# Taking the mean of a weight matrix from the float32 blocks as loaded, in a fused retention and expert kernel

## The chip, the cores and the metric

The kernel runs on one core of one Trainium2 chip. The metric is the device time of one execution in microseconds (us). The engines are called PE (TensorE, the matrix engine; PEld is its loading of weights), DVE (VectorE), ACT (ScalarE), POOL (GpSimd) and SP (SyncE, which here only issues transfers).

## The reference

Two stages. The first is a retention layer over q, k and v of 8 batches, 8 heads, 576 positions and 64 dimensions: scores with a causal decay mask, times v, no softmax. The second takes its output x (4608 tokens by 512) through an expert layer:

```python
scores = scale * np.matmul(q, k.transpose(0, 1, 3, 2))
ret = scores * Dmat[None, :, :, :]          # Dmat = gamma_h ** (i - j), causal
x = np.matmul(ret, v)                        # -> [4608, 512]
h = x @ w_in                                 # w_in 512 x 1024
e = np.exp(h - h_max)
solu = h * (e / np.sum(e))
ln = (solu - mu) / np.sqrt(var + 1e-06) * g_ln
out = ln @ w_out                             # w_out 1024 x 512
```

The subtraction of mu in front of w_out is folded into the weights: with W = g_ln * w_out (rows scaled), the kernel multiplies by W minus the mean of W over its 1024 rows. Finding this mean is what the change is about.

## The kernel before

The work is cut into 36 items i (a window of 256 positions by four heads, or the short last windows of four batches together) and 36 token tiles t of 128 tokens; two items make two tiles. Every step has a short name, and a number for its item, tile or block:

- SP: ldq, ldk, ldv load an item (256 KB each); lwi0 to lwi3 load the four blocks of w_in and lwo0, lwo2, lwo4, lwo6 the four double blocks of w_out (512 KB each) into a pool of five float32 buffers, wst; out stores a tile.
- sq, sk scale q and k by the decay into f16, cv casts v. They are on POOL, but for a few of the first items, which are on DVE or ACT.
- PE: T transposes q and k of an item, K multiplies k by v (the state), S makes the scores, I and V the output of the item. ACT copies T's result with Te (or TL) and the output with xe. DVE takes up the state with st and masks the scores with mask. POOL carries the state on with sm and sc.
- Tile t: M1 on PE (eight products into h_ps, one buffer of two PSUM banks), ex on ACT (exponential with its sum), so on DVE (h times e), L on PE (transposes), Le or TL on ACT, M2 on PE (eight products with w2c), oe on ACT, out. The statistics are bnA, bnB on DVE, or va on ACT with fin on DVE for the first four tiles; fx on ACT and rs on POOL make the factor of each row.
- Weights: wi0a to wi3b cast w_in into f16, half on ACT, half on DVE. For w_out, wg0 to wg7 make scaled f16 copies (g times the block), four on ACT (L714) and four on DVE (L710). WM (L720) multiplies them on PE by a constant f16 matrix `minus` of -1/1024, eight f16 products that add up in PSUM: every partition then holds minus the mean row. wc0 to wc7 on DVE (L728) read the float32 block again, scale it by g, add the mean from PSUM and write the centred f16 weights w2c over the scaled copies. M2_0 is the first that needs all eight wc. The PSUM bank of WM is that of the first four L (buffer `tl1[1]`), so L2 waits until the last wc has read it.

A setting of the plan, WE, says whether the mean is first copied from PSUM to SBUF by ACT (step wm, L724) and read from there by wc. It is 0 before:

```python
    op("WM", "PE", "WM", [f"wg{x}" for x in range(8)], (4, 1.3), [("tlL", ["wm"] if WE else [f"wc{x}" for x in range(8)])])
            op(f"wc{x}", "DVE", "wc", ["wm" if WE else "WM", f"lwo{c}"], (4, 0.1 * x))
```

The order on each engine is fixed in the program. A planner inside the kernel (plan, order_ops, with its own table of durations and due times) sorts the steps, and two tables, FIRST and LAST, give the order of the head and of the end by hand. PE's head before begins so:

```python
        "T0 S0 K0 K1 T1 I0 S1 V0 I1 V1 M1_0 K2 T2 T3 K3 S2 M1_1 I2 S3 V2 L0 I3 V3 T4 L1 K4 S4 M1_2 K6 WM K5 "
        "M1_3 T5 K7 T6 I4 S5 V4 T7 I5 S6 V5 T8 M1_4 I6 S7 V6 K8 T9 L2 M2_0 I7 L3 V7 K9 S8 M1_5 M2_1 I8 L4 V8 "
```

Where the planner expects PE to idle in the head, it puts in products of zeros (L846), 45 of them, which keep PE busy. At the end, cnt, cs and ci count the rows whose sum of exponentials lies in a safe range, and a branch on that count either finishes the last half tile or runs a general, slow version; with these data it is never the slow one.

Of the kernel before, what the change touches and what calls it, by code (L numbers as in the profile page):

```python
# [17 lines left out]
for _b in range(0, B, 4):  # L18
# [5 lines left out]
    T=0.26, L=0.26, Tw=0.45, Lw=0.45, I=0.22, V=0.23, K=0.13, S=0.22, M1=1.73, M2=1.73, M2h=0.87, oeh=0.42, G=0.1, WM=1.73,  # L24
# [3 lines left out]
    ldx=0.88, ldw=1.36, out=0.65,  # L28
# [4 lines left out]
NJ, NK, LAG, WE = 8, 8, 6, 0  # L33
VA = (0, 1, 2, 3)
ON = {'sq0': 'DVE', 'sq1': 'DVE', 'cv0': 'ACT', 'cv1': 'ACT', 'sk2': 'DVE', 'sk3': 'DVE', 'cv2': 'ACT', 'cv3': 'ACT', 'cv4': 'ACT', 'cv5': 'ACT', 'cv6': 'ACT', 'cv7': 'ACT'}
CAP = dict(
    rawq=5, rawk=5, rawv=5, q16=3, k16=4, v16=4, ev=8, s=1, ret=2, xy=1, gg=6, gt=2, s160=4, s161=9, h=1,
# [11 lines left out]
    ),  # L49
    ACT=(  # L50
# [4 lines left out]
    ),  # L55
    DVE=(
# [5 lines left out]
    ),  # L62
    POOL=(
# [4 lines left out]
    ),  # L68
    SP=(
# [13 lines left out]
        "oe27 xe34 ex32 Le30 Le31 oe28 xe35 ex33 fx15 oe29 ex34 Le32 oe30 Le33 oe31 fx16 ex35 oe32 Le34 oe33 "  # L83
        "Le35 fx17 oe34 oe35 oz"
    ),
    DVE=(
        "so31 mask35 bnA31 so32 bnB31 bnA32 so33 bnB32 so34 bnA34 bnA33 bnB33 bnB34 cnt so35 bnA35 ci bnB35"
# [5 lines left out]
        "out27 out28 out29 out30 out31 out32 out33 out34 out35"  # L93
# [28 lines left out]
def plan():  # L122
# [42 lines left out]
    for t in range(NT):  # L165
# [20 lines left out]
        op(f"L{t}", "PE", "Lw" if early else "L", [f"so{t}"] + after, (m + 2, 0.1),  # L186
# [5 lines left out]
        op(f"M2_{t}", "PE", "M2h" if end else "M2", need, (t + LAG, 3.1), [("h" if end else "xy" if late(t) and t % 2 else "s", [f"oe{t}"])])  # L192
# [116 lines left out]
def kernel(  # L309
# [44 lines left out]
    minus = const.tile([P, P], F16)  # L354
# [3 lines left out]
    se = const.tile([P, NT], FP)  # L358
# [222 lines left out]
    def mm1(t):  # L581
        w, c = divmod(t, 2)
        tk[t]["h"] = h_ps = pools["h"].tile([P, DFF], FP, tag="h", name="h_ps")
        for half in range(2):
            hh = slice(half * 512, half * 512 + 512)
            for dc in range(4):
# [5 lines left out]
    def exp_(t):
        d = tk[t]
        d["e"] = pools["e"].tile([P, DFF], FP, tag="e", name="e_sb")
        nc.scalar.activation(out=d["e"], in_=d["h"], func=ACT.Exp, accum_out=se[:, t : t + 1])  # L595

    def solu(t):
        d = tk[t]
        w, c = divmod(t, 2)
        d["solu"] = pools["solu"].tile([P, DFF], F16, tag="solu", name="solu")  # L600
        if c == 0:
            ws[w]["mv"] = pools["sml"].tile([P, 2, 2], FP, tag="mv", name="mv")
        if t in VA:
            d["su"] = pools["sml"].tile([P, 1], FP, tag="su", name="su")
            nc.vector.scalar_tensor_tensor(
                out=d["solu"], in0=d["h"], scalar=1.0, in1=d["e"], op0=ALU.mult, op1=ALU.mult,
                accum_out=d["su"],
            )
        else:
            nc.vector.tensor_tensor(out=d["solu"], in0=d["h"], in1=d["e"], op=ALU.mult)  # L610
# [9 lines left out]
    def squares(t):  # L620
# [4 lines left out]
            out=x, in_=d["solu"], func=ACT.Square, bias=d["su"], scale=-1024.0,  # L625
# [82 lines left out]
    def w2_cast(x, eng):  # L708
        if eng == "DVE":
            nc.vector.tensor_scalar(  # L710
                out=w2c16[:, x], in0=w2_f(x), scalar1=gln[:, x : x + 1], scalar2=None, op0=ALU.mult
            )
# [248 lines left out]
```

## Time and profile before

| | us |
|---|---|
| median of 3 runs | 213.53 (213.11 to 214.47) |
| the profiled execution, its own time | 212.58 |
| its span in the profile | 210.9 |
| PE busy | 200.8 (95%), 4400 instructions |
| DVE busy | 166.1 (79%) |
| ACT busy | 141.7 (67%) |
| POOL busy | 141.7 (67%) |
| of PE: products of zeros | 13.7 |
| first M1 / first M2 starts | 15.6 / 45.25 |

Rows of groups read: line, engine, operation, output<-inputs, shapes, count | busy us, mean ns of one | idle time of the engine before them. Rows of time read: start, length, engine, line, operation, with the idle time before it and what ended it in brackets. Rows of windows read: stretch, then busy time and number of instructions of each engine, the granted clock of PE, the share of the transfer engines and GB/s. In the slices, each digit is a fortieth of the span in tenths.

### The profile page before, as it was taken

To read this page: it belongs to the slowest core of one execution; us is meant where nothing else is said; L and a number is where in the kernel's file an instruction comes from. 1 tells how busy PE (TensorE), PEld (TensorE's weight loads), DVE (VectorE), ACT (ScalarE), POOL (GpSimd) and SP (SyncE) were. 2 spreads that over 40 slices of the span, in tenths; PEclk is the share of its full clock that TensorE was granted. 3 is DMA by queue.
4 is the path that set the end of the run, shared out by engine and by line. 5 is a ranking of instruction groups with operands and counts; after the bars stand their busy time and mean duration, and the time that the engine had idled before them with its cause. 6 is when DMAs were issued, how large, how long until landed. Compare 5 with 4: busy or idle time off the path is not lost. (4 is left out here: it accounts for less than half of the span.)

```text
span 210.9 us, 10171 instructions
## 1 busy us (share of the span) xinstructions
PE 200.8 (95%) x4400; PEld 113.2 (54%) x4400; DVE 166.1 (79%) x279; ACT 141.7 (67%) x235; POOL 141.7 (67%) x240
## 2 busy tenths in 40 slices
PE   7986989999999999999999999999999999999992
PEld 2442654665566555555555555555666555554451
DVE  6565779997868898978898898889988998753760
ACT  2375787897666776776666777666767777573752
POOL 7434758999997975948787979797979792001110
PEclk9999999999999999999999999999999999999999
DMA  5999999999666559778999686776355222311224
GB/s 157 345 355 334 329 311 269 301 293 306 195 188 188 169 139 278 217 214 259 314 288 305 198 252 183 217 234 181 94 152 153 54 57 67 71 63 54 101 101 104
DMA packets 64814, 42.66 MB, mean 202 GB/s; under 512 B 3320, under 2 KB 58624, under 8 KB 64768
## 3 DMA queue, kind: packets, MB, share of 16 engines
q1 hardware_dynamic: 64528, 41.82, 68.4%
q8 instruction: 34, 0.56, 1.2%
q10 hardware_dynamic: 240, 0.18, 0.5%
q14 instruction: 12, 0.10, 0.2%
HBM read 32.55 MB, written 9.44 MB: 199 GB/s over the span
## 5 line engine op out<-in xcount | busy, mean ns | idle before, releaser
L587 PE MATMUL h_ps<-w_in,xT 128*128 128x512 f16 x288 | 68.5, 380 | 0.0
L660 PE MATMUL o_ps<-w2c,ev 128*128 128x512 f16 (+1 forms) x296 | 67.6, 373 | 0.0
L610 DVE TENSOR_TENSOR solu<-h_ps,e_sb 128x1024 f16<-128x1024 f32 x32 | 39.2, 1223 | 16.7 <-ACT e_sb L595 16.5
L595 ACT ACTIVATE e_sb<-h_ps 128x1024 f32<-128x1024 f32 x36 | 36.8, 1023 | 21.9 <-PE h_ps L587 20.4
L540 DVE TENSOR_TENSOR ret<-s_ps,masks 128x1024 f16<-128x1024 f32 x36 | 43.9, 1220 | 6.0 <-PE s_ps L508 5.4
L660 PEld LDWEIGHTS <-ev 128*128 128x128 f16 x296 | 28.7, 98 | 32.7
L616 DVE BATCH_NORM_STATS2 bs<-solu 128x6 f32<-128x512 f16 x64 | 43.6, 685 | 0.9
L587 PEld LDWEIGHTS <-xT 128*128 128x128 f16 x288 | 25.3, 98 | 29.1 <-ACT xT L576 0.8
L394 POOL TENSOR_TENSOR q<-rawq,small 128x512 f16<-128x512 f32 x34 | 35.4, 1042 | 7.3 <-DMA rawq<-in_q_dram 5.9
L669 ACT ACTIVATE o_sb<-o_ps,rs 128x512 f32<-128x512 f32 (+1 forms) x37 | 25.0, 676 | 21.8 <-PE o_ps L660 10.4
L394 POOL TENSOR_TENSOR k<-rawk,small 128x512 f16<-128x512 f32 x34 | 35.4, 1042 | 6.0 <-DMA rawk<-in_k_dram 5.9
L457 ACT COPY ev<-tl 128x1024 f32<-128x1024 f32 (+1 forms) x32 | 29.7, 932 | 4.7 <-PE tl L429 4.2
L576 ACT CAST xT<-xy 128x512 f16<-128x512 f32 x36 | 26.7, 742 | 3.0 <-PE xy L472 2.9
L571 POOL CAST sbd<-gg 64x256 f16<-64x256 f32 x64 | 25.4, 397 | 3.0
L562 POOL TENSOR_TENSOR gg<-gt,small 128x128 f32<-128x128 f32 x32 | 13.1, 409 | 16.9 <-DVE gt L557 16.5
L648 POOL TENSOR_TENSOR w<-mv,w 128x2 f32<-128x2 f32 x16 | 3.1, 194 | 27.8 <-ACT w L633 13.9
L399 POOL CAST v<-rawv 128x512 f16<-128x512 f32 x28 | 17.1, 609 | 0.2
L508 PE MATMUL s_ps<-ev 64*64 64x128 f16 x576 | 14.8, 218 | 0.3
L472 PE MATMUL xy<-ret,v 64*64 64x128 f16 x576 | 14.7, 217 | 0.0
L472 PEld LDWEIGHTS <-sbd 128*128 128x128 f16 x128 | 9.3, 98 | 9.3 <-issue 1.1
L446 PE MATMUL tl<-ident,solu 64*64 64x64 f16 x1024 | 14.2, 195 | 0.0
L846 PE MATMUL tl<-zeros 128*128 128x512 f16 x41 | 12.7, 445 | 1.3 <-DVE zeros L802 1.3
(71 smaller groups left out, 214.6 us busy)
## 6 DMA issues: line engine op xcount, KB each, us to landing
rawq<-in_q_dram SPq DMA_DIRECT2D x32, 256.0 KB, 5.1
rawk<-in_k_dram SPq DMA_DIRECT2D x32, 256.0 KB, 5.3
rawv<-in_v_dram SPq DMA_DIRECT2D x32, 256.0 KB, 5.1
out_dram<-o_sb SPq DMA_DIRECT2D x26, 256.0 KB, 3.1
out_dram<-o_sb SPq DMA_DIRECT2D x19, 128.0 KB, 2.3
wst<-in_moe_w_in_dram SPq DMA_DIRECT2D x4, 512.0 KB, 6.8
wst<-in_moe_w_out_dram SPq DMA_DIRECT2D x4, 512.0 KB, 7.1
rawq<-in_q_dram SPq DMA_DIRECT2D x16, 64.0 KB, 2.4
```

The lines of the kernel that those rows point to most:

```text
L394: eng.tensor_tensor(out=t.rearrange("p j h d -> p h j d"), in0=st[i]["r" + nm], in1=g, op=ALU.mult)
L457: nc.scalar.copy(out=t[:, lo:hi].rearrange("p x (r w) -> p r x w", r=2), in_=tls[n].rearrange("p r x w -> p (r x w)").bitcast(FP).rearrang ...
L472: nc.tensor.matmul(start=(c, e) not in begun, stop=False, skip_group_check=True, **kw)
L540: nc.vector.tensor_tensor(out=d["ret"].rearrange("p e h j q -> p (e h) (j q)"), in0=d["s"].rearrange("p e h j q -> p (e h) (j q)"), in1=ma ...
L571: nc.gpsimd.tensor_copy(out=t[ee[e], :, :, ee[e]], in_=st[i]["gg"][ee[e]])
L576: nc.scalar.copy(out=xT[:, 2 * w : 2 * w + 2, 2 * hf : 2 * hf + 2].rearrange("p c h (q j) -> p c h j q", j=2), in_=xys[i][:, :, 0:256].rea ...
L587: nc.tensor.matmul(out=h_ps[:, hh], lhsT=xT[:, t, dc], rhs=w_in16[:, dc, hh], start=(dc == 0), stop=(dc == 3),)
L595: nc.scalar.activation(out=d["e"], in_=d["h"], func=ACT.Exp, accum_out=se[:, t : t + 1])
L610: nc.vector.tensor_tensor(out=d["solu"], in0=d["h"], in1=d["e"], op=ALU.mult)
L616: nc.vector.bn_stats(out=d["bs"][:, half], in_=d["solu"][:, half * 512 : half * 512 + 512])
L660: nc.tensor.matmul(out=o, lhsT=d["ev"][:, d["lo"] + c], rhs=w2c16[:, c, mm], start=(c == 0), stop=(c == 7))
L669: nc.scalar.activation(out=d["osb"][:, mm], in_=d["o", half], func=ACT.Copy, scale=ws[t // 2]["rs"][:, t % 2 : t % 2 + 1])
```

## The change

The scaled copies wg go, all eight, and so does the constant `minus`. In their place one DVE instruction, gn, writes a float32 matrix g_neg: for each of the eight blocks, g times -1/1024 repeated over 128 columns. WM becomes eight separate steps WM0 to WM7, each a float32 product of g_neg's block with the float32 block of w_out as loaded, so that each can run as soon as its own load has landed; they are spread over the head of PE's order. WE becomes 1: ACT copies the mean to SBUF (wm), and wc reads it there. cv8 and cv9 move from POOL to ACT. h_ps is now one fixed buffer with its two halves known to the plan. Code that splits the first tiles' M1, ex and so into halves comes in as well, with its settings at 0 (NH, HX, ND). All the hand-written orders are new: among others the w_out loads stand earlier in SP's, L2 and L3 earlier in PE's, so35 ahead of cnt at the end, and 33 products of zeros are left instead of 45. In the changed kernel's own numbering the lines are some 43 higher.

```diff
-NJ, NK, LAG, WE = 8, 8, 6, 0
+NH, HX, ND = 0, 0, 0
+NJ, NK, LAG, WE = 8, 8, 6, 1
+WO = (0, 2, 4, 6)
...
 FIRST = dict(
     PE=(
+        "K0 T0 S0 K1 T1 I0 S1 V0 I1 V1 M1_0 WM0 K2 WM1 T2 WM2 M1_1 WM3 K3 S2 T3 WM4 WM5 I2 S3 V2 T4 WM6 I3 S4 "
+        "V3 WM7 K4 M1_2 K5 T5 K6 L0 T6 I4 S5 V4 M1_3 S6 K7 L1 T7 I5 V5 L2 I6 S7 V6 K8 T8 M1_4 L3 T9 M2_0 I7 "
...
     ACT=(
+        "cv0 Te0 cv1 Te1 wi0a xe0 wi1a wi3a xe1 wi2a cv2 ex0 Te2 cv3 ex1 Te3 va0 xe2 Te4 cv4 xe3 wm cv5 cv6 "
...
     DVE=(
-        "sq0 sq1 st0 mask0 st1 wi1b mask1 wi2b wi3b wi0b sk2 sk3 st2 so0 st3 wg5 mask2 mask3 so1 st4 wg7 wg1 "
-        "wg3 mask4 st6 so2 st5 wc4 wc0 wc7 wc1 st7 so3 mask5 wc5 wc2 wc6 mask6 wc3 mask7 fin0 st8 so4 mask8 "
+        "sq0 st0 sq1 mask0 st1 wi0b mask1 wi3b gn wi2b wi1b sk2 st2 so0 sk3 st3 mask2 so1 mask3 mask4 st4 wc6 "
+        "wc2 st5 wc3 st6 so2 mask5 wc5 wc0 st7 wc4 mask6 so3 wc1 wc7 mask7 fin0 st8 so4 bnA4 mask8 st9 bnB4 "
...
     POOL=(
-        "sk0 sk1 sm0 sc0 sm1 sc1 sq2 sq3 sm2 sc2 sm3 sc3 sk4 sq4 sk6 sm4 sc4 sk5 sm6 sk7 sm5 sq5 sc5 sq6 sq7 "
-        "sk8 sq8 sk9 sc6 cv8 sq9 sm7 sc7 rs0 sq10 cv9 sq11 sm8 cv11 sk10 sc8 cv10 sk11 rs1 sm9 sc9 sq12 sm10 "
+        "sk0 sk1 sm0 sc0 sm1 sc1 sq2 sm2 sc2 sq3 sk4 sq4 sm3 sc3 sq5 sk5 sm4 sk6 sq6 sc4 sm5 sk7 sq7 sm6 sc5 "
+        "sc6 sq8 sk8 sm7 sk9 sq9 sc7 rs0 sm8 sq10 cv10 cv11 sc8 sq12 sk10 sq11 sk11 sm9 sk12 sc9 rs1 sm10 "
...
     SP=(
-        "ldq0 ldk0 ldv0 ldv1 ldq1 ldk1 lwi1 lwi2 lwi0 lwi3 ldk2 ldv2 ldq2 ldk3 ldq3 ldv3 lwo4 lwo0 ldk4 ldq4 "
-        "ldv4 lwo6 ldk6 lwo2 ldv6 ldk5 ldv5 ldk7 ldq5 ldv7 ldq6 ldk8 ldq7 ldq8 ldk9 ldv8 ldq9 ldq10 ldv9 "
+        "ldv0 ldk0 ldq0 ldk1 ldq1 ldv1 lwi0 lwi1 lwi3 lwi2 lwo0 ldk2 ldv2 ldq2 lwo2 ldv3 ldk3 ldq3 lwo4 ldk4 "
+        "ldq4 lwo6 ldv4 ldk5 ldq5 ldv5 ldv6 ldk6 ldq6 ldk7 ldq7 ldv7 ldq8 ldk8 ldv8 ldk9 ldq9 ldv9 ldq10 "
...
     DVE=(
-        "so31 mask35 bnA31 so32 bnB31 bnA32 so33 bnB32 so34 bnA34 bnA33 bnB33 bnB34 cnt so35 bnA35 ci bnB35"
+        "so31 bnA31 mask35 so32 bnB31 so33 bnA32 bnA33 so34 bnA34 bnB33 bnB32 bnB34 so35 cnt bnA35 ci bnB35"
...
-            op(f"wg{x}", "DVE" if x % 2 else "ACT", dict(DVE="wgD", ACT="wg"), [f"lwo{c}", "gc"], (1, 1.0 + 0.1 * x))
+    for n in range(8):
+        op(f"WM{n}", "PE", "WM", ["gn", f"lwo{WO[n // 2]}", f"WM{n - 1}" if n else ""], (3, 0.3 * n),
+           [] if n else [("tlL", ["wm"] if WE else [f"wc{x}" for x in range(8)])])
+    op("gn", "DVE", "gn", ["gc"], (-9999, 0.2))
...
-    minus = const.tile([P, P], F16)
+    g_neg = const.tile([P, 8, P], FP)
+    h_ps = pools["h"].tile([P, DFF], FP, tag="h", name="h_ps")
...
+    def g_neg_():
+        nc.vector.tensor_scalar(
+            out=g_neg, in0=gln[:, :, None].to_broadcast([P, 8, P]), scalar1=-1.0 / DFF, scalar2=None, op0=ALU.mult
+        )
...
-        for x in range(8):
-            nc.tensor.matmul(out=t, lhsT=minus, rhs=w2c16[:, x], start=(x == 0), stop=(x == 7))
+        x = WO[n // 2] + n % 2
+        nc.tensor.matmul(out=t, lhsT=g_neg[:, x], rhs=w2_f(x), start=(n == 0), stop=(n == 7))
```

More of the change, by code (lines that the diff above doesn't have):

```diff
@@ L32 @@
 OFF = 6.0
[L33 removed]
+NH, HX, ND = 0, 0, 0
+NJ, NK, LAG, WE = 8, 8, 6, 1
+WO = (0, 2, 4, 6)
 VA = (0, 1, 2, 3)
[L35 removed]
+ON = {'sq0': 'DVE', 'sq1': 'DVE', 'cv0': 'ACT', 'cv1': 'ACT', 'sk2': 'DVE', 'sk3': 'DVE', 'cv2': 'ACT', 'cv3': 'ACT', 'cv4': 'ACT', 'cv5': 'ACT', 'cv6': 'ACT', 'cv7': 'ACT', 'cv8': 'ACT', 'cv9': 'ACT'}
 CAP = dict(
[L37 removed]
+    rawq=5, rawk=5, rawv=5, q16=3, k16=4, v16=4, ev=8, s=1, ret=2, xy=1, gg=6, gt=2, s160=4, s161=9, ha=1, hb=1,
     e=2, solu=4, osb=3, tl=1, tlx=2, tlT=1, tlL=1, wst=5,
@@ L168, in plan @@
         va = t in VA
-        op(f"M1_{t}", "PE", "M1", [f"xe{2 * w}", f"xe{2 * w + 1}"] + [f"wi{x}{y}" for x in range(4) for y in "ab"], (m, 1.4), [("h", [f"so{t}"])])
-        op(f"ex{t}", "ACT", "ex", [f"M1_{t}"], (m, 3.3), [("e", [f"so{t}"])])
-        op(f"so{t}", "DVE", "soA" if va else "so", [f"ex{t}"], (m, 4.56), [("solu", [f"L{t}", f"va{t}" if va else f"bnB{t}"])])
+        xs = [f"xe{2 * w}", f"xe{2 * w + 1}"] + [f"wi{x}{y}" for x in range(4) for y in "ab"]
+        out = f"sp{t}" if t < NH else f"so{t}"
@@ L172, in plan @@
+        sums = t < HX or t < NH and va
+        if sums and c:
+            op(f"sg{w}", "POOL", "sg", ([f"ey{t - 1}", f"ey{t}"] if t < HX else []) + ([f"sp{t - 1}", f"sp{t}"] if va else []), (m, 4.9))
         if va:
-            op(f"va{t}", "ACT", "va", [f"so{t}"], (m + 1, 0.8))
+            op(f"va{t}", "ACT", "va", [f"sg{w}" if sums else out], (m + 1, 0.8))
         else:
-            op(f"bnA{t}", "DVE", "bnA", [f"so{t}"], (m + 1, 0.9))
+            op(f"bnA{t}", "DVE", "bnA", [out], (m + 1, 0.9))
@@ L218, in locks @@
 def locks(o):
-    return o.eng == "DVE" and o.name[:2] in ("sq", "sk", "cv", "wi", "wg")
+    return o.eng == "DVE" and o.name[:2] in ("sq", "sk", "cv", "wi", "gn")
 def parts(name):
@@ L579, in x_ev, with mm1 @@
         )
[L581 to L586, printed above, removed]
+    halves = [slice(0, 512), slice(512, 1024)]
+    def mm1(t, hs, dcs=range(4)):
+        for hh in hs:
+            for dc in dcs:
                 nc.tensor.matmul(
-                    out=h_ps[:, hh], lhsT=xT[:, t, dc], rhs=w_in16[:, dc, hh],
-                    start=(dc == 0), stop=(dc == 3),
-                )
@@ L592, in exp_ @@
[L592 to L597, printed above, removed]
+                    out=h_ps[:, hh], lhsT=xT[:, t, dc], rhs=w_in16[:, dc, hh], start=(dc == 0), stop=(dc == 3)
+                )
+    def exp_(t, half=0):
+        if not half:
+            tk[t]["e"] = pools["e"].tile([P, DFF], FP, tag="e", name="e_sb")
+        hh = halves[half] if t < HX else slice(0, DFF)
+        acc = part[:, 0, t, half : half + 1] if t < HX else se[:, t : t + 1]
+        nc.scalar.activation(out=tk[t]["e"][:, hh], in_=h_ps[:, hh], func=ACT.Exp, accum_out=acc)
@@ L598, in solu @@
+    def solu(t, half=0):
         d = tk[t]
         w, c = divmod(t, 2)
-        d["solu"] = pools["solu"].tile([P, DFF], F16, tag="solu", name="solu")
-        if c == 0:
-            ws[w]["mv"] = pools["sml"].tile([P, 2, 2], FP, tag="mv", name="mv")
+        if not half:
+            d["solu"] = pools["solu"].tile([P, DFF], F16, tag="solu", name="solu")
+            if c == 0:
+                ws[w]["mv"] = pools["sml"].tile([P, 2, 2], FP, tag="mv", name="mv")
+        hh = halves[half] if t < NH else slice(0, DFF)
@@ L612, in stats, with sums_of @@
+                accum_out=part[:, 1, t, half : half + 1] if t < NH else sums[:, 1, t : t + 1],
+            )
+        else:
+            nc.vector.tensor_tensor(out=d["solu"][:, hh], in0=h_ps[:, hh], in1=d["e"][:, hh], op=ALU.mult)
+    def sums_of(w):
+        nn = slice(0 if 2 * w < HX else 1, 2 if 2 * w in VA else 1)
+        tt = slice(2 * w, 2 * w + 2)
+        nc.gpsimd.tensor_tensor(out=sums[:, nn, tt], in0=part[:, nn, tt, 0], in1=part[:, nn, tt, 1], op=ALU.add)
     def stats(t, half):
@@ L655, in mm2 @@
         nm = "xy" if half or late(t) and t % 2 else "s"
-        nm = "h" if t == NT - 1 and not half else nm
         mm = slice(256 * half, 256 * half + (256 if t == NT - 1 else DM))
-        d["o", half] = o = pools[nm].tile([P, 2, 512], FP, tag=nm, name="o_ps")[:, 0, 0 : mm.stop - mm.start]
+        if t == NT - 1 and not half:
+            o = h_ps[:, mm]
+        else:
+            o = pools[nm].tile([P, 2, 512], FP, tag=nm, name="o_ps")[:, 0, 0 : mm.stop - mm.start]
+        d["o", half] = o
         for c in range(8):
@@ L700, in g_tp @@
     def g_tp():
-        cur["g"] = t = pools["h"].tile([P, DFF], FP, tag="h", name="g_ps")
-        nc.tensor.transpose(out=t[:, 0:8], in_=g_rows, identity=small[0:8, 70:78])
+        nc.tensor.transpose(out=h_ps[:, 0:8], in_=g_rows, identity=small[0:8, 70:78])
     def w_in_cast(c, half, copy):
@@ L745, in count_b, with dcs @@
     def count_b():
-        cur["cs"] = t = pools["h"].tile([P, DFF], FP, tag="h", name="cs")
-        nc.tensor.matmul(out=t[0:1, 0:1], lhsT=cur["n"], rhs=small[:, 68:69], start=True, stop=True)
+        nc.tensor.matmul(out=h_ps[0:1, 512:513], lhsT=cur["n"], rhs=small[:, 68:69], start=True, stop=True)
+    def dcs(t):
+        return range(2 if t < ND else 0, 4)
     def emit(o):
@@ L776, in emit @@
             w_load(x, w2_v)
-        elif k_ == "wg":
-            w2_cast(x, eng)
+        elif k_ == "gn":
+            g_neg_()
         elif k_ == "gc":
-            nc.vector.tensor_copy(out=gln, in_=cur["g"][:, 0:8])
+            nc.vector.tensor_copy(out=gln, in_=h_ps[:, 0:8])
         elif k_ == "cnt":
@@ L785, in emit @@
         elif k_ == "ci":
-            nc.vector.tensor_copy(out=count, in_=cur["cs"][0:1, 0:1])
+            nc.vector.tensor_copy(out=count, in_=h_ps[0:1, 512:513])
         elif name[:2] == "wi":
@@ L835 @@
             (lambda: tl1[1].bitcast(FP), busy([f"L{t}" for t in n_l], [f"Le{t}" for t in n_l])
-             + busy(["WM"], ["wm" if WE else max((f"wc{x}" for x in range(8)), key=start.get)])),
+             + busy(["WM0"], ["wm" if WE else max((f"wc{x}" for x in range(8)), key=start.get)])),
             (lambda: tl1[0].bitcast(FP), busy([f"T{i}" for i in n_t], [f"Te{i}" for i in n_t])),
```

80 lines of the change are left out of this document (46 added, 34 removed), and 32 rows, old and new, of tables (ACT, DVE, PE, POOL).

## The prediction

> **What bounds the kernel now.** I read the page first, then the windows, then the order of time around 28 and 44 us, then the groups kept apart by shape. The page's slices:
>
> ```profile
> span 210.9 us, 10171 instructions
> PE   7986989999999999999999999999999999999992
> POOL 7434758999997975948787979797979792001110
> PEclk9999999999999999999999999999999999999999
> DMA  5999999999666559778999686776355222311224
> ```
>
> TensorE (PE) is full from about the tenth slice to the end, at the full granted clock, so from there the time is PE's own work. Before that the DMA row is full (slices of 5.3 us, up to about 53 us) and PE is not. The windows give where the one takes over from the other; columns are PE, PEld, DVE, ACT, POOL:
>
> ```profile
> 15.00:20.00 5.00, 4.18 (x40) 1.80 (x38) 2.36 (x6) 3.43 (x6) 1.09 (x2) 1.00 1.16 318
> 25.00:30.00 5.00, 4.75 (x84) 3.07 (x82) 3.68 (x7) 4.33 (x10) 3.11 (x4) 1.00 1.12 326
> 35.00:40.00 5.00, 4.32 (x81) 2.65 (x80) 4.68 (x9) 4.61 (x10) 4.86 (x7) 1.00 1.07 287
> 40.00:45.00 5.00, 4.79 (x114) 3.33 (x114) 5.00 (x7) 4.62 (x10) 4.81 (x8) 1.00 1.18 294
> 45.00:50.00 5.00, 5.00 (x84) 3.04 (x82) 3.40 (x8) 4.06 (x8) 4.88 (x9) 1.00 1.17 297
> ```
>
> From 35 to 45 us DVE and POOL are the full ones; from 45 on PE is. The hand-over is one place:
>
> ```profile
> 43.25 1.04 POOL L394 TENSOR_TENSOR q<-rawq,small 128x512 f16<-128x512 f32 x1
> 44.34 0.40 PE L419 MATMUL tl<-ident,q 128*128 128x128 f16 x4 [0.19 <-POOL q L394]
> 45.25 1.89 PE L660 MATMUL o_ps<-w2c,ev 128*128 128x512 f16 x8
> ```
>
> POOL scales q of item 9 (sq9), PE transposes it (T9), then comes L2 and, at 45.25, M2_0. So what counts is **when M2_0 starts**: whatever delays it moves the end by as much, less the PE work that the new order has put ahead of it. The rest, M1_5 to the last store, is the same work at PE's pace.
>
> **The change, part by part.** Half-split code (NH, HX, ND) is all zero, so it adds nothing; the one fixed h_ps has the same users in the same order as the one-buffer pool. That leaves the mean, wc's source and the orders.
>
> Prices, from rows:
>
> ```profile
> L728 DVE SCALAR_TENSOR_TENSOR w2c<-wst,gln,tl 128x512 f16<-128x512 f32 x8 | 5.5, 739 | 0.0
> L714 ACT ACTIVATE w2c<-wst,gln 128x512 f16<-128x512 f32 x4 | 2.9, 730 | 0.8 <-DMA wst<-in_moe_w_out_dram 0.8
> L710 DVE TENSOR_SCALAR w2c<-wst,gln 128x512 f16<-128x512 f32 x4 | 2.4, 644 | 0.0
> L394 DVE TENSOR_TENSOR k<-rawk,small 128x512 f16<-128x512 f32 x2 | 1.4, 692 | 2.6 <-DMA rawk<-in_k_dram 2.5
> L747 PE MATMUL cs<-small,cn 128*1 128x1 f32 x2 | 0.2, 164 | 0.0
> ```
>
> Removed: wg, 2.9 us on ACT and 2.4 on DVE. Added: gn on DVE, 128x1024 from a broadcast; by the 0.42 us cast of 512 elements twice over, or the 1.22 us of a 1024-element product, 0.8 to 1.2, I take 1.1. It stands between wi3b and wi2b, so M1_0 starts at some 16.2 instead of 15.6. wm is one more 512-element copy on ACT (0.58, as L455's). cv8 and cv9 go from POOL (0.61) to ACT (0.62). In sum DVE -1.3, ACT -1.1, POOL -1.2.
>
> WM on PE was 8 x 0.216 = 1.73 (M1_4 starts at 41.33, the next work at 43.07: 1.74 for eight 128x512 f16). A float32 product of that width is not in the trace; L747 shows that one float32 product leaves two records. So it is 2 x 0.216 = 0.43 at the least, and 0.87 if each record streams twice-as-wide elements at half pace. I take 0.87, 6.9 us in all; the low end is 3.5. The Trainium skill, FP8 and Floating Point Precision, TensorE Precision Notes, says that true FP32 takes four passes, which would come to the same 0.86. Most of it lies in gaps: PE's idle and warm-up fills of 15 to 30 us are 2.0 + 3.7 us there, and items 3 and 4 arrive later now (next).
>
> The SP order is what moves the data. Count loads in units of 256 KB (a weight load is two). Waits that ended on a landing in the trace: 17th unit 17.6 us, 19th 19.95, 25th 24.5, 30th 28.4, 34th 31.6, 36th 33.3: some 0.83 each. All four loads of w_out move forward, so q2 goes from the 17th to the 19th, q3 from 19th to 24th (23.4), q4 from 26th to 28th (27.0), lwo6, the last weights, are the 30th (28.4), k5 32nd, q5 from 37th to 33rd (30.7), q6 37th (34.2). By q9 both orders have loaded 45 units.
>
> POOL, in its new order with 1.04 a scaling, 0.4 an sm, 0.85 an sc: sq2 from 19.95, sq3 23.4, sk4 26.1, sq4 to 28.2, sm3, sc3, then sq5 at 30.7 and dense: ten scalings, three sm (1.2) and three sc (2.5) up to sk9, then sq9 with sm7, ending at 45.4. Before it was 44.3: the earlier weights cost POOL 1.1 us.
>
> PE and DVE: WM0 follows M1_0 (17.7 to 18.6); K2 waits for v2 to 19.6; T2 for sq2 to 21; M1_1 22.4; WM3, K3, S2, T3, WM4, WM5 run to 27.6; V2 waits for mask2, T4 at 28.4, WM6 28.85, WM7 ends 31.3. ACT: wm to 32.1. M1_2 starts at 31.65 (28.7 before), waiting for xe3. DVE then is dense: st4 to 32.45, wc6, wc2, st5 (34.45), wc3, st6, so2 (to 37.05), mask5, wc5, wc0, st7, wc4, mask6 (to 42.2), so3 (43.45). M1_3 waits for so2 and starts at 37.1, M1_4 waits for so3: 43.5. L3, then T9 at 45.75, M2_0 at 46.2; wc7 is done at 44.9, in time. Against 45.25 that is +0.95. Work taken ahead of M2_0 is L3 (L2 already was), about -0.35. **Sum without anything new: +0.6.** What sits behind each late so on DVE is the next mask, and behind that S and V on PE.
>
> **The new cost: wc beside POOL.** Before, wc read its mean from PSUM; now both of its tensors are in SBUF. What DVE and POOL do to each other shows at wg (DVE, three in a row) against POOL:
>
> ```profile
> 28.43 1.04 POOL L394 TENSOR_TENSOR k<-rawk,small 128x512 f16<-128x512 f32 x1 [1.89 <-DMA rawk<-in_k_dram]
> 28.89 1.94 DVE L710 TENSOR_SCALAR w2c<-wst,gln 128x512 f16<-128x512 f32 x3
> 29.43 0.58 POOL L562 TENSOR_TENSOR gg<-gt,small 128x128 f32<-128x128 f32 x1
> 30.08 1.01 POOL L571 CAST sbd<-gg 64x256 f16<-64x256 f32 x2
> ```
>
> An undisturbed wg took 0.48, the longest of these 0.865: it ended only after POOL's product was through (29.47). In turn POOL's 0.40 product took 0.58 and its 0.83 pair of casts 1.01. They take turns, one instruction at a time. The wc rows (736 to 741 ns, all eight) show that with a PSUM source there were no turns. No DVE operation with two SBUF tensors overlaps a POOL one in this trace: the four scalings on DVE (0.69) ran while POOL waited for data. So the price is between nothing and full turns. Full turns: from 32.45 on I let each wc wait for the running POOL instruction and hold the next one 0.6. wc6 to 33.4, wc2 34.4, wc3 36.0, so2 to 37.85, wc5 39.9, wc0 41.55, wc4 43.0, so3 45.45, M1_4 47.0 behind sk8 (46.4), wc7 48.0, sk9 49.05, sq9 50.1, M2_0 50.6: +4.4 on the 46.2. The DVE's mean penalty at wg, 0.17 an instruction, times 8 would be +1.4. I take 3 of the 4.4, nearer the full turns, since wc holds POOL for longer than wg did, and not all since some will meet POOL waiting for a landing. The Trainium skill, GPSIMD Engine Reference, Specifications, lists contention with DVE instructions "in a 2-port perf mode or with two SBUF inputs". By that sentence wc pays now and did not before, as the wc rows agree; the sum by it is the full-turn one.
>
> **Sum.** +0.6 + 3 = +3.6 us. Against the profiled execution (212.58, of which 210.9 is the span and 1.7 lies around it, unchanged) 216.2; the median shown is 213.53, 0.95 higher, so 217.0 against it, which is the number I give. Tail: cnt now stands after so35 but L35 waited for PE (M2_33, to 202.4), not so35, so nothing.
>
> **Rivals.**
> A. *No turns with two SBUF sources.* The 0.69 rows are as short as an undisturbed operation can be, but nothing ran beside them. Then +0.6, with a landing's jitter of 1 us each way: 213 to 215, say 214.1.
> B. *The relief decides, and it is faster.* Place: the gate sq9 to T9. With cv8 gone from POOL, and if the landings do not hold sq3 to sq5 back as counted (a microsecond less at sq5 suffices), sq9 ends at 43.7, M2_0 comes straight after T9 at 44.2 (L2 and L3 being done), -1.05 and -0.35: -1.4, and with float32 products at the low price and mask6 and so3 a wc earlier, up to -2.7: 210.8 to 212.1. It decides only if so3 ends before 42.4; for it speaks that DVE and ACT have 2.4 us less to do, against it that DVE has more behind the mean than before.
> C. *wc itself becomes slow.* If two float32 streams run at half pace, wc gains another 0.5 (512 elements are worth 1.22 - 0.74 = 0.48 between the 1024- and the 512-element rows), 0.69 becomes about 1.2, and DVE, dense from 32 to 45, gains 8 x 0.5 = 4 us on top: 221. The only speed of two SBUF streams in the rows, 0.69, speaks against it. The Trainium skill, Vector Engine (DVE) Microarchitecture Reference, Points that are easy to get wrong, does say that this form with two non-bf16 SBUF sources halves throughput; no run here shows it.
>
> **How the numbers follow.** Forecast 0.52, A 0.25, B 0.13, C 0.10. The range 212.3 to 220 leaves out most of B and C. About 1% (2.1 us) is what a measurement of this kernel can tell from no change. Faster by more: most of B, 0.10. Within: A, the rest of B and the forecast's low edge (+1.4 + 0.6), 0.32. Slower: 0.58.
>
> **What would show it.** wc over 0.85 us on DVE at many of its eight, and POOL scalings over 1.04 between 32 and 48 us: the turns. M1_2 near 31.6, M1_4 near 46 to 47, M2_0 near 49, against 43.5 and 46.2 for A. Eight float32 products with 0.87 each on PE between 17 and 32. wc at 0.69 throughout and M2_0 before 45.6 would prove me wrong, and so would PE going idle after M2_0, which would mean a second bound.

## The result

The changed kernel takes 216.55 us (median of 6 runs, 215.38 to 219.31), the kernel before 212.82 (211.96 to 214.47) beside it. The ratio is 1.014, with a 95% interval of 1.010 to 1.019; it leaves out two disturbed runs of the changed kernel (218.8 and 219.3 us), and so it is below the quotient of the medians. So it is slower by 1.4%, some 3 us; 217.0 was forecast against a median before of 213.53, which is +3.5. The profiled execution took 216.02 us, of which 214.2 are the span: +3.4 on the 212.58 of the one before.

### The profile after

The page's head and slices:

```profile
span 214.2 us, 10157 instructions
PE   7999997879999999999899999999999999999991
POOL 8524469999987999656959788797979793010110
PEclk9999999999999999999999999999999999999999
```

PE is as full as before from about the tenth slice on, and at the full clock. The time was lost ahead of that, where the windows show POOL full, DVE nearly so, and PE waiting (columns PE, PEld, DVE, ACT, POOL):

```profile
40.00:45.00 5.00, 3.40 (x95) 2.60 (x95) 4.96 (x8) 3.42 (x8) 4.76 (x8) 1.00 1.16 294
45.00:50.00 5.00, 4.79 (x44) 2.85 (x41) 4.35 (x9) 3.97 (x8) 4.86 (x8) 1.00 1.10 284
```

From 40 to 45 us PE has 3.40 of 5 where it had 4.79 before. POOL is as busy as before, but with longer instructions. The order of time, with DVE, POOL and PE together:

```profile
30.19 1.04 POOL L428 TENSOR_TENSOR q<-rawq,small 128x512 f16<-128x512 f32 x1 [1.53 <-PE xy L506]
...
32.05 1.55 DVE L767 SCALAR_TENSOR_TENSOR w2c<-wst,gln,w_m 128x512 f16<-128x512 f32 x2
32.22 0.84 POOL L596 TENSOR_TENSOR gg<-gt,small 128x128 f32<-128x128 f32 x1
33.02 1.49 POOL L428 TENSOR_TENSOR k<-rawk,small 128x512 f16<-128x512 f32 x1
...
38.63 1.95 DVE L767 SCALAR_TENSOR_TENSOR w2c<-wst,gln,w_m 128x512 f16<-128x512 f32 x2
39.98 2.55 POOL L605 CAST sbd<-gg 64x256 f16<-64x256 f32 x4
...
46.87 1.04 POOL L428 TENSOR_TENSOR q<-rawq,small 128x512 f16<-128x512 f32 x1
47.97 0.40 PE L453 MATMUL tl<-ident,q 128*128 128x128 f16 x4 [0.21 <-POOL q L428]
48.42 1.89 PE L703 MATMUL o_ps<-w2c,ev 128*128 128x512 f16 x8
```

These are the turns. A pair of wc takes 1.55 to 1.98 us on DVE (1.40 undisturbed, in experiment 2). On POOL the sm beside it takes 0.84 instead of 0.40, the scaling 1.49 instead of 1.04, and the four casts of sc5 and sc6 2.55 instead of 1.75: some 0.44 us for each wc. M2_0 still hangs on sq9 and T9, and starts at 48.42 instead of 45.25: +3.17. For the wait ahead of sq5 (30.19) the profile names PE. By the plan sq5 waits only for the landing of q5 and for a buffer that T2 had given free by 20.7 us, so it is read here as the landing, which the profile does name in experiments 2, 3, 6 and 7.

What becomes of this shows in ex, tile by tile: +3.06 at tile 5, +2.49 at tile 15, +3.11 at tile 16, +3.09 at the last. So 0.68 of M2_0's delay is given back, as it would be by work already done; a wait of PE then takes 0.63 again:

```profile
106.29 0.29 PE L463 MATMUL tl<-ident,q 64*64 64x64 f16 x13 [0.94 <-issue]
```

For this wait the profile shows no releaser. Before, one of 0.31 us stood near the same place. That the delay of M2_0 and that of the end agree is therefore in part luck.

### The profile page after: what moved, and what is told of

Its sections match the earlier page's. It is cut to its first block, busy times and chain, and to the rows that moved or that the text cites. A ratio compares the mean times of both kernels' runs of the same rounds, so it can differ in the third digit from the quotient of the medians.

```text
span 214.2 us, 10157 instructions
## 1 busy us (share of the span) xinstructions
PE 203.5 (95%) x4396; PEld 114.1 (53%) x4396; DVE 166.6 (78%) x275; ACT 140.1 (65%) x234; POOL 143.7 (67%) x238
## 5 line engine op out<-in xcount | busy, mean ns | idle before, releaser
L703 PE MATMUL o_ps<-w2c,ev 128*128 128x512 f16 (+1 forms) x288 | 66.9, 376 | 0.0
L656 DVE BATCH_NORM_STATS2 bs<-solu 128x6 f32<-128x512 f16 x64 | 43.7, 686 | 0.9
L428 POOL TENSOR_TENSOR q<-rawq,small 128x512 f16<-128x512 f32 x34 | 35.9, 1055 | 10.1 <-DMA rawq<-in_q_dram 7.7
L428 POOL TENSOR_TENSOR k<-rawk,small 128x512 f16<-128x512 f32 x34 | 36.3, 1068 | 3.5 <-DMA rawk<-in_k_dram 2.1
L712 ACT ACTIVATE o_sb<-o_ps,rs 128x512 f32<-128x512 f32 (+1 forms) x36 | 24.5, 681 | 20.9 <-PE o_ps L703 11.0
L605 POOL CAST sbd<-gg 64x256 f16<-64x256 f32 x64 | 26.0, 407 | 3.0
L596 POOL TENSOR_TENSOR gg<-gt,small 128x128 f32<-128x128 f32 x32 | 14.6, 456 | 14.8 <-DVE gt L591 14.3
L688 POOL TENSOR_TENSOR w<-mv,w 128x2 f32<-128x2 f32 x16 | 3.1, 194 | 30.7 <-DVE mv L658 13.1
L433 POOL CAST v<-rawv 128x512 f16<-128x512 f32 x26 | 15.7, 609 | 0.1
L690 POOL TENSOR_TENSOR rs<-w,small 128x2 f32<-128x2 f32 x18 | 12.4, 690 | 1.4
```

What stands on the lines that cost most here:

```text
L428: eng.tensor_tensor(out=t.rearrange("p j h d -> p h j d"), in0=st[i]["r" + nm], in1=g, op=ALU.mult)
L605: nc.gpsimd.tensor_copy(out=t[ee[e], :, :, ee[e]], in_=st[i]["gg"][ee[e]])
L656: nc.vector.bn_stats(out=d["bs"][:, half], in_=d["solu"][:, half * 512 : half * 512 + 512])
L703: nc.tensor.matmul(out=o, lhsT=d["ev"][:, d["lo"] + c], rhs=w2c16[:, c, mm], start=(c == 0), stop=(c == 7))
L712: nc.scalar.activation(out=d["osb"][:, mm], in_=d["o", half], func=ACT.Copy, scale=ws[t // 2]["rs"][:, t % 2 : t % 2 + 1])
```

## The experiments

The theory was that the turns between wc and POOL make most of the loss and the earlier weights the rest. The rivals were that the float32 products on PE make it, or the landings alone, or that POOL's chain, which sets M2_0, is governed by something else.

**1. Turns put into the kernel before.** One switch and the copy of the mean; nothing else is changed.

```diff
-NJ, NK, LAG, WE = 8, 8, 6, 0
+NJ, NK, LAG, WE = 8, 8, 6, 1
-        "wg6 wg2 cv6 ex2 cv5 va1 cv7 ...
+        "wg6 wg2 cv6 ex2 cv5 wm va1 cv7 ...
```

> The kernel before, all its orders kept, with one thing changed: the mean goes to SBUF (wm on ACT, put between cv5 and va1) and wc reads it there. Turns theory (wc with two SBUF tensors and POOL take turns): POOL instructions beside a wc grow by some 0.45 us each, as they do in the changed kernel, seven or eight of them ahead of sq9, so M2_0 starts at 47.5 to 48.5 instead of 45.25 and the time is 2 to 3.5 us above the kernel before. Rival (new orders and transfers carry the loss, wc's source is free): wc at 0.74, POOL rows as before, within 0.5 us of the kernel before, or faster by up to 0.5 since L2 no longer waits for the last wc.

Measured: 218.24 us against 213.02, ratio 1.023 (1.019 to 1.027). The order of time, first the kernel before and then with the switch:

```profile
34.34 2.71 DVE L728 SCALAR_TENSOR_TENSOR w2c<-wst,gln,tl 128x512 f16<-128x512 f32 x4
34.50 0.40 POOL L562 TENSOR_TENSOR gg<-gt,small 128x128 f32<-128x128 f32 x1 [0.20 <-DVE gt L557]
34.86 1.04 POOL L394 TENSOR_TENSOR q<-rawq,small 128x512 f16<-128x512 f32 x1
```

```profile
34.29 3.80 DVE L728 SCALAR_TENSOR_TENSOR w2c<-wst,gln,w_m 128x512 f16<-128x512 f32 x4
34.45 0.84 POOL L562 TENSOR_TENSOR gg<-gt,small 128x128 f32<-128x128 f32 x1
35.25 1.49 POOL L394 TENSOR_TENSOR q<-rawq,small 128x512 f16<-128x512 f32 x1
...
48.95 1.89 PE L660 MATMUL o_ps<-w2c,ev 128*128 128x512 f16 x8 [0.61 <-DVE ret L540]
...
117.95 0.25 PE L446 MATMUL tl<-ident,solu 64*64 64x64 f16 x7 [1.44 <-issue]
```

Four wc that took 2.71 us before take 3.80, and the same two POOL instructions are longer by 0.44 and 0.45. So reading the mean from SBUF slows this kernel by itself. M2_0 starts 3.7 us later (48.95), a little past the expected 47.5 to 48.5. Of that, 2.93 are POOL's chain (sq9 at 46.18 instead of 43.25). The rest comes after T9, where PE waits 0.61 us for DVE: mask7, whose PSUM buffer M2_0 uses, stands behind the last wc and ends at 48.90. The eight wc took 8.71 us in all instead of 5.50, so here the turns cost on DVE too. The price in time, some 5 us, is above the expected 2 to 3.5: another 1.44 us is the wait of PE without a releaser.

**2. Turns taken out of the changed kernel.** wc reads the mean from PSUM again. Since WM and the first four L share a bank, L0 to L3, and their copies on ACT, then have to come after the last wc: after T9.

```diff
-NJ, NK, LAG, WE = 8, 8, 6, 1
+NJ, NK, LAG, WE = 8, 8, 6, 0
-        "V3 WM7 K4 M1_2 K5 T5 K6 L0 T6 ... M1_3 S6 K7 L1 T7 I5 V5 L2 ... M1_4 L3 T9 M2_0 I7 "
-        "L4 V7 K9 S8 M1_5 M2_1 I8 ...
+        "V3 WM7 K4 M1_2 K5 T5 K6 T6 ... M1_3 S6 K7 T7 I5 V5 ... M1_4 T9 L0 I7 M2_0 L1 "
+        "V7 L2 K9 S8 L3 M1_5 M2_1 L4 I8 ...
```

> The changed kernel with the mean left in PSUM (no wm, wc reads PSUM) and, since that holds the bank, L0 to L3 put behind the last wc and around M2_0; everything else, float32 products and new orders, stays. Turns theory: wc 0.74 each, POOL products back at 1.04, M1_4 starts near 43.5 (45.4 in the changed kernel), T9 near 45 (47.97). L0 to L3 then cost PE some 1.4 us of four transposes after that point, so the time is about 1 to 2.5 us under the changed kernel, 214 to 215.5. Rival (orders or float32 products carry the loss): T9 stays near 47.5 to 48 and the time rises by the 1.4 us of L, to 217.5 to 218.

Measured: 217.23 us against 213.02, ratio 1.020 (1.016 to 1.025). That misses the expected 214 to 215.5, though POOL does what was expected:

```profile
30.79 1.04 POOL L428 TENSOR_TENSOR q<-rawq,small 128x512 f16<-128x512 f32 x1 [1.96 <-DMA rawq<-in_q_dram]
...
38.97 1.75 POOL L605 CAST sbd<-gg 64x256 f16<-64x256 f32 x4
44.17 1.05 POOL L428 TENSOR_TENSOR q<-rawq,small 128x512 f16<-128x512 f32 x1
45.34 0.39 PE L453 MATMUL tl<-ident,q 128*128 128x128 f16 x4
47.67 1.90 PE L703 MATMUL o_ps<-w2c,ev 128*128 128x512 f16 x8 [0.85 <-ACT ev L489]
```

Every POOL instruction has its undisturbed length, and T9 comes 2.63 us earlier than in the changed kernel. But L0 now stands behind T9, M2_0 waits for it, and M1_5 starts at 53.28 (51.50 in the changed kernel): what the turns cost was paid once more by the late L.

**3. No turns, with the L placed better.** As 2, with this order of PE, and the copies on ACT moved to fit it, Le0 ahead of ex4:

```diff
-M1_4 T9 L0 I7 M2_0 L1 V7 L2 K9 S8 L3 M1_5 M2_1
+M1_4 L0 T9 I7 L1 M2_0 V7 L2 K9 S8 M1_5 L3 M2_1
```

> The changed kernel without turns (mean read in PSUM by all eight wc), with L0 to L3 set better than in the first such version: L0 and L1 around T9, M2_0, then L2 and L3, and their copies on ACT ahead of the exponential. Turns theory: POOL rows and wc undisturbed, M1_4 near 43.6; with L0 ahead of it T9 near 45.8, M2_0 near 47, M1_5 near 50.5 (51.5 in the changed kernel, 48.4 before): 215 to 216, 0.5 to 1.5 us under the changed kernel and 1 to 2.5 above the kernel before. Rival (turns are worth nothing to the end): as the first PSUM version, 217 or more.

Measured: 214.89 us against 212.98, ratio 1.010 (1.007 to 1.013). M2_0 starts at 47.75 and M1_5 at 50.95. So without turns and with fitting orders, 1.0% of the 1.4% is still there; the two intervals overlap, so the times alone don't even show a gain. The trace shows where the turns' worth went. Against the changed kernel M2_0 is 0.67 us earlier: POOL's chain is 3.43 shorter, but sq5 started 1.35 later with the same order of loads, and from sq9 to M2_0 it is 2.96 instead of 1.55, since L0, I7 and L1 now stand in between.

**4. Half the turns.** Blocks 2, 3, 5 and 0 read the mean in PSUM, the other four in SBUF; L0 to L2 stand behind wc0 and ahead of T9.

```diff
+IN_PS = (2, 3, 5, 0)
...
-            out=..., in1=cur["w_mean"], ...
+            out=..., in1=cur["w_mean" if x in IN_PS else "w_m"], ...
```

> The changed kernel with a half dose: wm stays, but four of the eight wc (2, 3, 5, 0) read the mean from PSUM and four (6, 4, 1, 7) from SBUF; L0 to L2 move behind wc0, still ahead of T9, L3 behind M2_0. Turns theory: only the four with two SBUF tensors lengthen a POOL instruction (by 0.45 each), the other four take 0.74; T9 starts about half way between 45.3 (no turns) and 47.97 (eight turns), 46.3 to 47.0, and the time is 0.5 to 1.5 us under the changed kernel. Rival (the gain of the PSUM version at T9 came from L0 to L3 being out of the way, not from the turns): T9 stays at 47.5 or later, since L0 to L2 are ahead of it here.

Measured: 215.05 us against 212.98, ratio 1.011 (1.008 to 1.015). T9 starts at 46.66. Both are as expected, though this interval too overlaps that of the changed kernel (1.010 to 1.019).

**The turns measured by the chain of POOL.** sq5 to sq9 is a dense chain on POOL, the same steps in experiments 2 to 4, 6 and 7 and in the changed kernel. From the start of sq5 to the start of sq9:

| | wc with two SBUF tensors | sq5 | sq9 | between |
|---|---|---|---|---|
| changed kernel | 8 | 30.19 | 46.87 | 16.68 |
| 4, half | 4 | 30.51 | 45.57 | 15.06 |
| 2, none | 0 | 30.79 | 44.17 | 13.38 |
| 3, none | 0 | 31.54 | 44.79 | 13.25 |

Experiments 6 and 7, with eight, have 16.81 and 16.68. Eight such wc lengthen the chain by 3.3 to 3.4 us and four by 1.7 to 1.8. So the price goes with the number, 0.41 to 0.45 us each, in one trace of each kernel.

**5. The relief of POOL that rival B counted on.** In the kernel before, cv8 goes from POOL to ACT; nothing else.

```diff
-    ... "sk8 sq8 sk9 sc6 cv8 sq9 sm7 ...        # POOL
+    ... "sk8 sq8 sk9 sc6 sq9 sm7 ...
-    ... Te7 xe5 va0 Te8 ...                     # ACT
+    ... Te7 xe5 cv8 va0 Te8 ...
```

> The kernel before with cv8 alone moved from POOL to ACT, as the change does. Theory (sq9 on POOL is the gate to the full PE): sq9 ends 0.6 us earlier, T9 follows K8 at once (44.0 to 44.1 instead of 44.34), M2_0 near 44.8 to 45.0: 0.2 to 0.5 us faster, hard to tell from nothing in the times, seen in the trace. Rival (DVE's last wc or ACT is the gate): M2_0 at 45.2 or later, no gain or a loss of up to 0.5.

Measured: 212.93 us (12 runs) against 212.98, ratio 1.001 (0.999 to 1.004): no difference, a miss. In its trace POOL waits 0.78 us ahead of sq7 for a T on PE, and sq9 ends at 44.1 instead of 44.3. The 0.6 us taken off POOL became a wait. M2_0 starts at 45.51, where the rival put it (45.2 or later). The last wc isn't what held it, it is done by 43.6; but DVE is, with the step behind: M2_0 uses the PSUM buffer that mask7 reads, and mask7 ends at 45.46. In the kernel before mask7 ends at 45.12, ahead of M2_0 at 45.25. So right behind sq9 stands a second gate there.

**6. Only two float32 products.** WM0 and WM7 stay; the other six blocks are left out of the mean.

```diff
     def WM_(n):
+        if 0 < n < 7:
+            return
```

> The changed kernel with only the first and the last of the eight float32 products (so the mean leaves six blocks out): six products at 0.885, 5.3 us of PE work, are gone from 17 to 31 us. Turns theory (POOL's chain from the landing of q5 on is the gate): M1_2 starts up to 1 us earlier, the POOL chain hardly moves, the time is 0 to 0.7 us under the changed kernel. Rival (the dearer products on PE carry the loss): the time is 2 to 3.5 us under it.

Measured: 216.83 us against 213.02, ratio 1.016 (1.010 to 1.022). It isn't faster than the changed kernel, but the windows show something else that changed:

```profile
30.00:35.00 5.00, 5.00 (x50) 1.93 (x49) 3.09 (x6) 2.78 (x5) 4.09 (x4) 0.71 1.02 279
```

The granted clock fell to 0.71 from 30 to 35 us, after PE had been busy only 2.71 of 5 us where the products had been. The float32 product that was left there, WM7, took 2.07 us instead of 1.12. So this run tests two things at once; experiment 7 keeps PE busy there.

**7. Cheap products in the place of six.** Each of the six is replaced by two f16 products of zeros, so the six blocks are left out here too.

```diff
+        if 0 < n < 7:
+            for _ in range(2):
+                nc.tensor.matmul(out=t, lhsT=zeros[:, :P], rhs=zeros, start=False, stop=False)
+            return
```

> The changed kernel with each of the six inner float32 products replaced by two f16 products of zeros that add nothing (so the mean leaves six blocks out): PE keeps working there and keeps its clock, at 0.43 instead of 0.885 a product, 2.7 us of PE work less. Theory (the products lie in gaps, POOL's chain with its turns is the gate): T9 within 0.4 us of the changed kernel's 47.97, the time 0 to 0.6 us under it, POOL rows still stretched. Rival (the price of the float32 products is on the path): 1.5 to 2.7 us under the changed kernel.

Measured: 217.97 us against 213.29, ratio 1.023 (1.020 to 1.026): slower than the changed kernel by the ratios, not faster, and why the median is higher is open. The mean granted clock of its runs is 0.984 to 0.999, against 0.998 to 1.000 in the four runs of the changed kernel that its ratio counts, but that doesn't explain it: the run with 0.999 took 218.36 us, and the quickest, 215.72, had 0.988. In its profiled execution (216.72 us, full clock up to 150 us) POOL's order of time reads:

```profile
30.60 1.04 POOL L428 TENSOR_TENSOR q<-rawq,small 128x512 f16<-128x512 f32 x1 [1.78 <-DMA rawq<-in_q_dram]
...
47.28 1.04 POOL L428 TENSOR_TENSOR q<-rawq,small 128x512 f16<-128x512 f32 x1
```

M1_2 does start 0.35 us earlier (30.97). But sq5 waits for the landing of q5, and from there it is 16.68 us to sq9 again, to the digit. M2_0 follows sq5 by 18.23 us in the changed kernel, 18.24 here and 18.36 in experiment 6. So in the changed kernel's order the six float32 products aren't on the path to M2_0: the start of sq5 and POOL's chain are. That rests on the traces; the times only show no gain.

**8. The float32 mean in the orders of before.** Here the products have no gaps made for them: four stand in a row ahead of M1_3; WE is 0, cv8 and cv9 are back on POOL.

```diff
-        ... M1_1 I2 S3 V2 L0 I3 V3 T4 L1 K4 S4 M1_2 K6 WM K5 M1_3 ...
+        ... M1_1 WM0 WM1 I2 S3 V2 WM2 WM3 I3 V3 T4 K4 S4 M1_2 K6 WM4 WM5 WM6 WM7 K5 M1_3 ...
```

> The new mean alone: the old orders of SP, POOL and of the rest, eight float32 products spread from behind M1_1 to ahead of M1_3 in the order in which their blocks land, no scaled copies, mean left in PSUM; since its bank is held from the first product on, L0 to L3 stand behind the last wc. Theory: no turns, DVE is relieved of 2.4 us and ACT of 2.9, the gate stays sq9 at 44.3; the last block lands at 29.75, so the products end near 33 as WM did, M1_3 near 33.7 to 35; L0 to L3 after 44 instead of L2 and L3 cost PE 0.9 and some waits for their copies: 213.5 to 216. Rival (the float32 products on PE carry a loss): M1_3 starts at 36 or later, 217 or more. Rival (relief decides): under 212.5.

Measured: 219.89 us against 212.98, ratio 1.035 (1.031 to 1.038). The row ahead of M1_3:

```profile
32.55 3.70 PE L758 MATMUL tl<-wst,g_neg 128*128 128x512 f32 x8
```

Four products there take 3.70 us; M1_3 starts at 36.44 instead of 33.68. M2_0 then waits 0.72 us for ACT and starts at 48.90. Here the rival holds: the products cost time where PE has no gap for them. The late L are in this loss too (L0 to L3 stand behind the last wc, as in experiment 2), so it isn't the products' price alone.

**9 and 10. The order of the loads.** Experiment 9 gives the changed kernel the old SP order for the weights and items 0 to 7 (and WO the old sequence). Experiment 10 gives the kernel before the earlier loads of w_out, with no other edit; the planner answers them with other products of zeros.

```diff
-        "... lwi0 lwi1 lwi3 lwi2 lwo0 ldk2 ldv2 ldq2 lwo2 ldv3 ldk3 ldq3 lwo4 ...     # 9
+        "... lwi1 lwi2 lwi0 lwi3 ldk2 ldv2 ldq2 ldk3 ldq3 ldv3 lwo4 lwo0 ldk4 ...
-        "... lwi3 ldk2 ldv2 ldq2 ldk3 ldq3 ldv3 lwo4 lwo0 ldk4 ldq4 ldv4 lwo6 ...     # 10
+        "... lwi3 lwo4 ldk2 ldv2 ldq2 lwo0 ldk3 ldq3 ldv3 lwo6 ldk4 ldq4 ldv4 lwo2 ...
```

> The changed kernel with the loads of the weights and of items 0 to 7 in the order of the kernel before, and the float32 products taken in the order in which their blocks then land (4, 0, 6, 2). Prediction's step (the earlier weights cost POOL 1.1 us by holding back sq3 to sq5): 0.3 to 1.2 us under the changed kernel, unless the last block, landing near 29.8 instead of 28.4, delays wm and wc by a microsecond and gives that back. Turns theory alone expects the wc and POOL rows to stay stretched here. Rival (the transfer order carries the whole loss): 2.5 us or more under the changed kernel.

> The kernel before with only the four w_out loads moved forward in SP's order, in the changed kernel's manner (one ahead of each of items 2, 3, 4, the last ahead of k6). Theory (a load moved ahead holds every later one back by two units of 0.83 us, and the gate is POOL's chain): sq3 some 3 us later, sk4 and sq4 1.6, sk6 1.6, sq9 0.4 to 1.1 us later, time 0.3 to 1.3 us above the kernel before. Rival (earlier weights cost nothing since POOL idles there): sq9 and the time unchanged within 0.3. Rival (earlier weights help, as DVE starts its wc sooner): 0.3 to 1 us faster.

Measured: experiment 9 223.69 us against 213.02, ratio 1.050 (1.045 to 1.055); experiment 10 216.33 against 213.29, ratio 1.014 (1.010 to 1.019). Both are misses. Experiment 9 was expected below the changed kernel and is far above it, and experiment 10, with some 3 us, is above its 0.3 to 1.3. In 9 the first float32 product waits for its block in PE's order, and all behind it:

```profile
22.28 1.39 PE L755 MATMUL tl<-wst,g_neg 128*128 128x512 f32 x2 [2.67 <-DMA wst<-in_moe_w_out_dram]
```

So 9 doesn't measure what the landings cost. In 10, DVE's second scaling waits for k3:

```profile
22.16 0.69 DVE L394 TENSOR_TENSOR k<-rawk,small 128x512 f16<-128x512 f32 x1 [4.04 <-DMA rawk<-in_k_dram]
```

It started at 18.92 before. The 3.2 us are four units of 256 KB at the predicted 0.83, the two w_out loads ahead of it. sq3 on POOL is as late, and ends at 24.21. But M1_1 is later still, 26.18 instead of 22.08, and that is PE:

```profile
21.53 3.79 PE L846 MATMUL tl<-zeros 128*128 128x512 f16 x9
```

The planner put nine products of zeros ahead of T3, where four had stood before. They ran while the granted clock was 0.66 (20 to 25 us). T3 starts at 25.16, straight behind them and some 0.9 us after sq3, then K3, S2 and M1_1. sq9 ends 3.2 us later than before, and M2_0 starts 3.2 later; how much of the 0.9 is in that wasn't separated. The trace is of an execution of 218.07 us, the longest of the six.

In experiment 2, which has the w_out loads as early but cv8 and cv9 off POOL and new orders throughout, sq9 ends only 0.9 later. So part of what earlier weights cost here is spared by orders made for them; how much, these two runs don't show.

No version was faster than the kernel before. The best with the new mean are experiments 3 and 4, which the times can't tell apart.

## Why the prediction was right, point by point

- **What sets the time.** sq9, T9, M2_0, as predicted (in the kernel before, mask7 on DVE is a second gate 0.1 us behind, see experiment 5); M2_0's +3.17 and the span's +3.3 agree, in part by luck (see L3 below). The +3.17 is, from the traces: +0.92 at sq9 without turns (experiment 2 against before), +3.30 for the turns, -0.60 since sq5 started earlier than in experiment 2, and -0.45 between sq9 and M2_0, where L2 no longer stands.
- **The walk without turns.** sq5 was put at 30.7 and the end of sq9 at 45.4. Experiment 2 has 30.79 and 45.2. The prediction's sum counts "ten scalings" up to sk9, but sq9 is the tenth: added up from its own prices it gives 45.25. The count of landings in 256 KB units held for sq3 and sq5; sq2 and sk4 came 0.6 to 0.9 us earlier than counted.
- **The turns.** 3 us were taken out of a full-turn walk of 4.4 at M2_0; POOL's chain shows 3.3 to 3.4. The full-turn walk was too long because it let wc hold the next POOL instruction 0.6 us; it is 0.42 to 0.44, and pairs of wc took 1.55 to 1.98 rather than 2 to 2.5. So M1_4 started at 45.41 instead of 46 to 47.
- **M2_0 "near 49", measured 48.42.** From the 46.2 without turns: sq5 0.5 earlier than predicted, the chain without turns 0.4 shorter (13.3 for 13.7), and 0.25 less between sq9 and M2_0, since L3 ran while PE waited; plus 3.35 for the turns: 48.4. The early sq5 is luck: in the five other kernels with this order of loads it started at 30.51 to 31.54. So terms that were a few tenths off in both directions cancelled, and the hit of the number is closer than the terms are.
- **L3 as work taken ahead, -0.35.** Too small, and lost: 0.68 is given back between M2_0 and tile 15, and the wait of 0.94 us at 106 (0.31 before) takes 0.63 again. That wait isn't in the prediction. Experiments 2 to 4 show none; why is open.
- **Prices.** A float32 product was taken at 0.87. In PE's order of time two stand back to back (four records), and the next work starts 1.77 us after the first, so it is 0.885 each:

```profile
25.10 1.94 PE L759 MATMUL tl<-wst,g_neg 128*128 128x512 f32 x4
26.87 0.39 PE L506 MATMUL xy<-ev,sbd 128*128 128x128 f16 x4
```

  PE's fills of 15 to 30 us were read as 3.7 us; the windows have 2.4 (0.19 and 0.59 from 20 to 30). The sum doesn't hang on it, since the walk placed each product by itself. gn was put too high, at 1.1; its row has 0.69, at 13.99, and M1_0 started at 15.86 instead of 16.2. The row of wc by source (count: least/median/most in ns, from when to when):

```profile
L767 DVE SCALAR_TENSOR_TENSOR w2c<-wst,gln,w_m x8: 743/886/1173, 32.1 to 45.1; 128x512 f16<-128x512 f32 x8
```

- **Rival A (no turns)** falls by the POOL rows and by the table.
- **Rival B (the relief decides).** It needed sq9 to end at 43.7. Even without turns it ended at 45.2 (experiment 2), and so3, which was to end before 42.4, ended at 43.1 there and at 44.1 in the changed kernel. Experiment 5 adds that in the kernel before 0.6 us less on POOL turned into a wait.
- **Rival C (half pace for two SBUF streams)** falls by the last row: the shortest wc, 743 ns, is as long as with the mean in PSUM (736 to 741). The Trainium skill, Vector Engine (DVE) Microarchitecture Reference, Points that are easy to get wrong, says that this form halves throughput with two non-bf16 SBUF sources; the 743 ns do not agree, and the measurement decides.
- **The turns and the notes.** The Trainium skill, GPSIMD Engine Reference, Specifications, lists contention for DVE instructions with two SBUF inputs. Experiments 1 to 4 and 8 agree, experiment 1 by one switch: 0.44 us a wc on POOL with the mean in SBUF, nothing with it in PSUM.

What the result is made of: the turns lengthen POOL's chain by 3.3 us, but reading the mean from PSUM ties L0 to L3 to the last wc, and that cost 1.4 us of it again in experiment 3; another 1.35 went with a late sq5. So taking the turns out brought 1.010 against 1.014, with overlapping intervals, and not the 1.5% that 3.3 us would be. That the turns delay M2_0 is shown; what the changed kernel would take without them and without the tie of the L is not shown by any run. The other 1.0% is in the orders and the mean: sq9 ends 0.9 us later than before in experiment 2 and 1.5 in experiment 3, where sq5 also came latest. These were not split further.

## What to carry to other kernels

When an operand moves from PSUM to SBUF on DVE, look at what POOL does beside it, not at the instruction's own length: here DVE's work was the same undisturbed, and each such instruction held a full POOL queue up by 0.42 us. Beside POOL it also grew itself, from 743 ns to as much as 1173. Measure along the chain that sets the end, from one of its fixed steps to the next: sq5 to sq9 told three doses apart, where the medians were blurred by landings and orders. An order of engines written for one set of landings isn't good for another: new orders with old loads lost 5.0%, and old orders with the w_out loads moved forward 1.4%, as much as the whole change. And where a planner fills idle time by itself, an edit to the loads is not an edit to the loads alone.

## What the runs showed of the hardware that was not expected

- Without most of the float32 products PE was busy 3.26, 3.70 and 2.71 us in the three stretches of 5 us from 15 to 30, and the granted clock was 0.95 in the last of these and 0.71 in the next; with cheap products in their place it was busy 3.72 to 4.32, and the clock stayed at 1.00 throughout. The clock also fell in experiment 5 (0.66 from 10 to 15 us, after 3.72 of 5), experiment 9 (0.80 and 0.86 from 20 to 30, PE busy 2.72 in the first) and experiment 10 (0.66 from 20 to 25, after 3.53 of 5). In the changed kernel 3.40 of 5 from 40 to 45 us left it at 1.00, so the busy time of a stretch doesn't decide it alone.
- The same SP order let sq5 start between 30.19 and 31.54 us in six kernels. In the three with the changed kernel's orders that spread goes into M2_0 whole: M2_0 follows sq5 by 18.23 to 18.36 us.
- PE stood without a visible releaser for 0.31 to 1.44 us near 103 to 118 us in five of the kernels.
